# Carrying a batch's sums to all partition quadrants by sixteen SBUF-to-SBUF transfers instead of matmuls

## The chip, the cores and the metric

One Trainium2 (trn2) chip, one core. The metric is the device time of one execution in microseconds (us). Each kernel was run several times, in the same rounds and on the same chip as the kernel before; medians are quoted with the lowest and highest run. A program on one core shows a mean granted TensorE clock for each run, as a share of full speed.

## The reference

A polynomial-sketch attention feeds a SwiGLU feed-forward block. Cut to what matters:

```python
# q, k, v: (4 batches, 4 heads, 1088 positions, 32), float32; S1, S2: (8, 32)
def phi(x):                                  # 64 features per position and head
    a = einsum('rd,bhsd->bhsr', S1, x)
    b = einsum('rd,bhsd->bhsr', S2, x)
    return einsum('bhsi,bhsj->bhsij', a, b).reshape(..., 64)
q_p, k_p = phi(q), phi(k)
kv  = einsum('bhsf,bhsd->bhfd', k_p, v)      # per batch: values' sums, 64 x 32 per head
z   = sum(k_p, axis=2)                       # per batch: features' sums, 64 per head
num = einsum('bhsf,bhfd->bhsd', q_p, kv)
den = einsum('bhsf,bhf->bhs', q_p, z)[..., None] + 1e-06
x   = (num / den) as (4352, 128)
g, val = x @ w_gate, x @ w_val               # 128 -> 1536
out = (silu(g) * val) @ w_out                # 1536 -> 128
```

`kv` and `z` of a batch need all its positions, so nothing of `num` and `den` can start before them. `S1`, `S2` and the three weights reach the kernel as 64-bit numbers (the 8 x 32 values of `S1` are a load of 2 KB); the kernel turns them into float32 itself, which is called narrowing below.

## The kernel before

The feed-forward part is the bulk of the work. A block of 384 or 320 positions and one of 12 chunks of 128 hidden columns is a *unit*: two matmuls (`g`, `u`), a silu on ScalarE, a multiplication on VectorE (`hj`). A down-projection follows two units later. `g` and `u` take their PSUM banks from a rotation.

```python
    free_banks = ["g0", "g1", "g2", "acc"]
    turn = [0]
    def bank(tag=None):
        if tag is None:
            tag = free_banks[turn[0] % len(free_banks)]
            turn[0] += 1
        return psum.tile([P, TB], FP32, tag=tag, name="bank")
    # ... (cut)
    def unit(i, j, late=False):
        t0, n = blocks[i]
        g, u = bank(), bank()
        for o, w in ((g, wg), (u, wv)):
            nc.tensor.matmul(o[:, 0:n], w[:, j, :], xT[:, t0 : t0 + n], start=True, stop=True)
        # ... (cut) sg = silu(g) on ScalarE; hj = sg * u on VectorE, or on GpSimd for late ones
```

While the units of batch b run, the attention of batch b + 1 is worked off beside them, as a generator: after each unit it gets one turn, up to its next `yield`. This is the part that is changed, in the middle of it:

```python
        zs = feature_sums(phk)                       # sums over the position chunks, GpSimd
        # ... (cut: three yields)
        kvz = wide("a")
        key_values(kvz[:, 0, :], phk, 0, NC)         # kv: head h on partitions 32h..32h+31
        nc.tensor.matmul(kvz[:, 1, 0 : H * F], ones[:], zs, start=True, stop=True)  # z, 128 wide
        kvs = apool.tile([P, 2, 4, 32], FP32, tag="kvs", name="kvs")
        zrep = apool.tile([P, H * R, R], FP32, tag="zrep", name="zrep")
        nc.scalar.copy(kvs[:], ...)                  # kv, repeated four times
        nc.scalar.copy(zrep[:], ...)
        # ... (cut: load of the next batch's v)
        yield
        kvp = wide("b")[:, 0, 0 : 2 * P].rearrange("p (g n) -> p g n", g=2)
        for g in range(2):                           # turned and carried to all quadrants
            nc.tensor.matmul(kvp[:, g, :], kvs[:, g, :, :].rearrange("p a f -> p (a f)"),
                             ident[:], start=True, stop=True)
        kvr = apool.tile([P, 2, P], FP32, tag="kvr", name="kvr")
        nc.scalar.copy(kvr[:], kvp)
        # ... (cut) VectorE: zrep times query factors, sums, 1/den, query features, transpose phT
        # ... (cut) TensorE: num[quadrant] from kvr and phT;  copies of num into xT
```

In the last section of the first batch the rotation loses its fourth bank, which becomes the accumulator of the down-projections:

```python
    for z, (i, j) in enumerate(seq):
        if z == 17:
            free_banks.pop()
        unit(i, j)
        # ... (cut)
```

## Time and profile before

| | kernel before |
|---|---|
| time, median of 4 runs | 310.79 us (310.68 to 312.23) |
| span of the profiled run | 308.8 us |
| mean granted TensorE clock | 1.0 |
| TensorE busy | 302.3 us, 98% |

A line of the timeline gives start, duration, engine, source line, operation, names and shapes, and in brackets the idle time ahead of it with what ended that. A matmul's printed duration includes its modelled end, so read its pace from the next start. This is the timeline of the kernel before at the place of the change, in the first of the three later batches:

```profile
72.29 1.21 PE L312 MATMUL a<-phk,vld 128*32 128x64 f32 x72
73.43 0.70 PE L529 MATMUL a<-zs,ones 128*128 128x256 f32 x2
...
75.69 0.61 PE L543 MATMUL b<-ident,kvs 128*128 128x128 f32 x4
...
76.33 0.38 ACT L548 COPY kvr<-b 128x256 f32<-128x256 f32 x1 [1.18 <-PE b L543]
76.39 0.92 DVE L559 TENSOR_TENSOR phq<-zrep,qab 128x768 f32<-128x768 f32 x1
```

From the sums' end (73.97) to VectorE's first product with them (76.39) it takes 2.4 us, and TensorE never stands for it.

### The profile page before, as it was taken

Reading aid. Unit: us, or ns where it says so; the run is one execution under the profiler, and the core shown is the slowest. Engines: PE = TensorE matmul, PEld = TensorE weight load, DVE = VectorE, ACT = ScalarE, POOL = GpSimd, SP = SyncE. Lnnn points to the kernel's source line nnn. Section 1 sums busy time; section 2 is a strip of 40 time slices with the busy share of each in tenths; the row PEclk is TensorE's granted clock in tenths of the full one; section 3 lists DMA queues with packets and bytes.
Section 4 is the critical chain, followed back from the end, with each engine's and each line's share of the span. In section 5 each row is a group of like instructions: output and inputs, shape, how many; then the busy total and the mean of one; then the engine's idle time right before and its main releaser. Section 6 shows DMA issues by size and latency. Waiting matters only on the chain.

```text
span 308.8 us, 5147 instructions
## 1 busy us (share of the span) xinstructions
PE 302.3 (98%) x2066; PEld 191.1 (62%) x2066; DVE 175.7 (57%) x332; ACT 96.4 (31%) x227; POOL 37.3 (12%) x54
## 2 busy tenths in 40 slices
PE   8899999999999999999999999999999999999994
PEld 7545555656565566666666656655676655676664
DVE  4897999653659556279944552897532323333321
ACT  3556665223002313222232232322222222222230
POOL 3226223244000002400000032000000000000000
PEclk9999999999999999999999999999999999999999
DMA  7564390402111040220100100100010100100101
GB/s 197 165 168 104 103 318 0 146 0 70 31 28 21 2 132 14 34 66 0 27 2 0 24 1 2 25 0 0 11 17 0 21 2 1 25 0 1 22 0 26
DMA packets 24663, 13.96 MB, mean 45 GB/s; under 512 B 18368, under 2 KB 22720, under 8 KB 24640
## 3 DMA queue, kind: packets, MB, share of 16 engines
q1 hardware_dynamic: 23712, 13.28, 17.0%
q10 hardware_dynamic: 928, 0.36, 0.5%
q8 instruction: 16, 0.26, 0.4%
q14 instruction: 7, 0.06, 0.1%
HBM read 11.41 MB, written 2.23 MB: 44 GB/s over the span
## 4 chain that ended last, share of the span: by engine, by line
PE 89%; DVE 6%; ACT 2%; issue 1%; DVEq 0%
PE bank L652 50%; PE bank L680 28%; DVE hj L666 2%; PE bank L195 2%; DVE exp L225 1%; PE a L603 1%; PE a L278 1%; PE a L312 1%; DVE man L229 1%; PE b L278 1%; DVE exp L217 1%; PE a L694 1%; ACT exp L222 1%; PE a L529 1%; PE bank L325 0%
## 5 line engine op out<-in xcount | busy, mean ns | idle before, releaser
L666 DVE TENSOR_TENSOR hj<-sg,bank 128x384 f32<-128x384 f32 (+1 forms) x138 | 72.7, 528 | 102.3 <-PE bank L652 101.3
L658 ACT ACTIVATE sg<-bank 128x384 f32<-128x384 f32 (+1 forms) x144 | 67.8, 473 | 155.4 <-PE bank L652 155.4
L652 PE MATMUL bank<-xT,wg 128*128 128x384 f32 (+1 forms) x288 | 112.9, 474 | 0.0
L652 PE MATMUL bank<-xT,wv 128*128 128x384 f32 (+1 forms) x288 | 111.7, 469 | 0.3 <-DVE wv L238 0.3
L680 PE MATMUL bank<-hj,wo 128*128 128x384 f32 (+2 forms) x288 | 105.2, 460 | 0.2 <-DVE hj L666 0.2
L652 PEld LDWEIGHTS bank<-xT,wv 128*128 128x128 f32 x288 | 54.1, 190 | 34.5 <-DVE hj L666 2.7
L680 PEld LDWEIGHTS bank<-hj,wo 128*128 128x128 f32 x288 | 54.4, 190 | 32.9 <-issue 0.7
L652 PEld LDWEIGHTS bank<-xT,wg 128*128 128x128 f32 x288 | 53.1, 190 | 31.5 <-issue 2.4
L475 POOL TENSOR_TENSOR zs<-phk 128x1024 f32<-128x1024 f32 x3 | 7.0, 2349 | 111.9 <-PE bank L652 104.2
L566 DVE TENSOR_REDUCE dot<-phq 128x96 f32<-128x768 f32 x9 | 13.8, 1531 | 0.0
L301 DVE TENSOR_TENSOR phk<-kas,a 128x512 f32<-128x512 f32 (+1 forms) x12 | 8.7, 749 | 5.2 <-ACT kas L510 5.2
L708 DVE STREAM_TRANSPOSE o<-bank 128x384 f32<-128x384 f32 (+2 forms) x12 | 6.6, 548 | 6.9 <-PE bank L680 6.6
L222 ACT ACTIVATE exp<-exp,rebias 128x384 int32<-128x384 int32 (+3 forms) x15 | 8.3, 552 | 5.2 <-DVE exp L217 4.6
L590 DVE STREAM_TRANSPOSE phT<-phq 128x768 f32<-128x768 f32 x9 | 8.7, 967 | 0.1
L301 DVE TENSOR_TENSOR phq<-qab 128x768 f32<-128x768 f32 x9 | 8.5, 948 | 0.0
L559 DVE TENSOR_TENSOR phq<-zrep,qab 128x768 f32<-128x768 f32 x9 | 8.5, 942 | 0.0
L225 DVE SCALAR_TENSOR_TENSOR exp<-raw,exp 128x384 int32<-128x384 int32 (+2 forms) x14 | 7.4, 528 | 0.4 <-ACT exp L222 0.4
L621 ACT COPY xT<-a 128x64 f32<-128x64 f32 (+4 forms) x9 | 2.4, 333 | 15.8 <-PE b L603 9.5
L229 DVE SCALAR_TENSOR_TENSOR man<-raw,man 128x384 f32<-128x384 uint32 (+2 forms) x14 | 7.1, 511 | 0.0
L223 ACT ACTIVATE man<-man 128x384 f32<-128x384 int32 (+3 forms) x15 | 6.7, 450 | 0.0
L217 DVE TENSOR_SCALAR exp<-raw 128x384 int32<-128x384 int32 (+2 forms) x14 | 6.4, 457 | 0.5 <-DMA raw<-in_moe_w_val_dram 0.5
L263 DVE STREAM_TRANSPOSE kT<-kld 128x384 f32<-128x384 f32 (+2 forms) x9 | 6.1, 692 | 0.3 <-DMA kld<-in_k_dram 0.3
(113 smaller groups left out, 162.6 us busy)
## 6 DMA issues: line engine op xcount, KB each, us to landing
kld<-in_k_dram SPq DMA_DIRECT2D x4, 544.0 KB, 4.1
vld<-in_v_dram SPq DMA_DIRECT2D x12, 144.0 KB, 4.8
qld<-in_q_dram SPq DMA_DIRECT2D x3, 544.0 KB, 3.4
raw<-in_moe_w_out_dram SPq DMA_DIRECT2D x4, 384.0 KB, 4.0
out_dram<-o SPq DMA_DIRECT2D x28, 48.0 KB, 1.8
raw<-in_moe_w_gate_dram SPq DMA_DIRECT2D x3, 384.0 KB, 3.3
raw<-in_moe_w_val_dram SPq DMA_DIRECT2D x3, 384.0 KB, 3.4
out_dram<-o SPq DMA_DIRECT2D x16, 40.0 KB, 1.7
```

The source lines that it names most:

```text
L217: nc.vector.tensor_scalar(e[:], hi, 0x7FF00000, None, op0=ALU.bitwise_and)
L222: nc.scalar.activation(e[:], e[:], AF.Relu, bias=rebias[: shape[0], :], scale=8.0)
L225: nc.vector.scalar_tensor_tensor(out=e[:], in0=hi, scalar=-(1 << 31), in1=e[:], op0=ALU.bitwise_and, op1=ALU.bitwise_or,)
L229: nc.vector.scalar_tensor_tensor(out=f, in0=lo, scalar=2.0**-52, in1=f, op0=ALU.mult, op1=ALU.add)
L301: engine.tensor_tensor(out=phk[:, c0:c1, :, :, :].rearrange("p c h i j -> p (c h) i j"), in0=ka.unsqueeze(3).to_broadcast([P, n, R, R]), i ...
L559: nc.vector.tensor_tensor(out=prod, in0=zrep[:].unsqueeze(1).to_broadcast([P, n, H * R, R]), in1=fac.unsqueeze(3).to_broadcast([P, n, H * ...
L566: nc.vector.tensor_reduce(out=dot[:, x, :], in_=phq[:, c0:c1, :, :, :].rearrange("p c h i j -> p (c h) j i"), axis=AX.X, op=ALU.add,)
L590: nc.vector.transpose(out=phT[:, :, :, c0:c1, :].rearrange("p h g c t -> p c (h g) t"), in_=phq[:, c0:c1, :, :, :].rearrange("p c h (g i) ...
L652: nc.tensor.matmul(o[:, 0:n], w[:, j, :], xT[:, t0 : t0 + n], start=True, stop=True)
L658: nc.scalar.activation(sg[:, 0:n], g[:, 0:n], AF.Silu)
L666: nc.vector.tensor_tensor(out=hj[:, 0:n], in0=sg[:, 0:n], in1=u[:, 0:n], op=ALU.mult)
L680: nc.tensor.matmul(acc[i][:, 0:n], wo[:, j, :], hidden[i, j][:, 0:n], start=(j == 0), stop=(j == NCH - 1),)
```

## The change

The intent: TensorE is the bound, so take the carrying off it. The features' sum is made per head on 32 output columns and lands beside `kv`. VectorE turns `kv`, and sixteen transfers on the SyncE queue copy each head's sums to each of the four partition quadrants. To give these time, the attention waits four turns instead of one. In the first batch fewer warm-up matmuls on constants run (`keep_warm`), a mask and a matmul are put earlier, the later narrowing of weights is spaced wider, and the weight loads move from ScalarE's queue to SyncE's. The last output leaves in four transfers instead of two.

```diff
-        nc.tensor.matmul(kvz[:, 1, 0 : H * F], ones[:], zs, start=True, stop=True)
-        (kvs, zrep and their two ScalarE copies)
+        for h in range(H):
+            nc.tensor.matmul(
+                kvz[32 * h : 32 * h + 32, 1, 0:F], ones[:], zs[:, F * h : F * h + F],
+                start=True, stop=True,
+            )
+        kz4 = apool.tile([P, 2, F], FP32, tag="kz4", name="kz4")
+        spread = apool.tile([P, 2, H, F], FP32, tag="spread", name="spread")
+        nc.scalar.copy(kz4[:, 0, :], kvz[:, 1, 0:F])
+        nc.vector.transpose(
+            out=kz4[:, 1, :].rearrange("p (g d) -> p g d", g=2),
+            in_=kvz[:, 0, 0:F].rearrange("p (g f) -> p g f", g=2),
+        )
+        for a in range(4):
+            for h in range(H):
+                nc.sync.dma_start(
+                    out=spread[32 * a : 32 * a + 32, :, h, :],
+                    in_=kz4[32 * h : 32 * h + 32, :, :],
+                )
-        yield
-        (the two carrying matmuls and the copy to kvr)
+        for _ in range(4):
+            yield
 ... (cut: zrep and kvr become views of spread)
 first batch:
-    keep_warm(16, 32, ps=ps)
+    keep_warm(7, 32, ps=ps)
-    for _ in range(2):
-        load_next(nc.scalar)
 ... (cut: all these loads on SyncE now)
-    nd = totals(steps[1][1], phq, kvz, side_by_side("b"))
-    part("wv", 1)
-    unit(0, 1, late=True)
+    nd = side_by_side("b")
+    turn[0] = 2
+    unit(0, 1, late=True, between=(lambda: totals(steps[1][1], phq, kvz, nd), None))
-        z += z // 2 * 3
-        for at in (z, z + 1, z + 2 + z % 5):
+        z += z // 2 * 4
+        for at in (z, z + 1, z + 2 + z % 6):
 ... (cut: one more warm-up matmul, xT's layout for the last block, the last output)
```

More of the change, by code (lines that the diff above doesn't have):

```diff
@@ L137, with load_next @@
     coming += [("wo", i) for i in range(len(pieces["wo"]))]
-    def load_next(queue=nc.sync):
+    def load_next():
         if not coming:
@@ L149, in load_next @@
         if not wide_w:
-            queue.dma_start(out=dst[:, c0:c1, :], in_=part)
+            nc.sync.dma_start(out=dst[:, c0:c1, :], in_=part)
             return
         t = raw[name, i] = stage.tile([P, 3, P], I64, tag="raw", name="raw", bufs=NRAW)
-        queue.dma_start(out=t[:, 0 : c1 - c0, :], in_=part)
+        nc.sync.dma_start(out=t[:, 0 : c1 - c0, :], in_=part)
     nc.sync.dma_start(out=sraw[0:R, :], in_=S1)
@@ L168 @@
     ident = const.tile([P, P], FP32, name="ident")
-    ones = const.tile([P, P], FP32, name="ones")
+    ones = const.tile([P, Dh], FP32, name="ones")
     own = const.tile([P, H], FP32, name="own")
@@ L326, in unit_sums @@
                 kz[32 * a : 32 * a + 32, 0 : H * F],
-                ones[:, 0:Dh],
+                ones[:],
                 phk[:, c, :, :, :].rearrange("p h i j -> p (h i j)"),
@@ L459, in divide @@
             todo = [(xs, nd[0][:, :, 0:w].rearrange(deep, t=32), rs)]
-        if t0 == blocks[LAST][0]:
-            m = SPLIT // 64
-            ys = xT[:, t0 + SPLIT : t0 + BW].rearrange("p (t x a) -> p a x t", a=2, t=32)
-            _, num, r = todo.pop()
-            todo = [(xs[:, :, 0:m], num[:, :, 0:m], r[:, :, 0:m]), (ys, num[:, :, m:], r[:, :, m:])]
         for x, num, r in todo:
@@ L528, in attention @@
         key_values(kvz[:, 0, :], phk, 0, NC)
-        nc.tensor.matmul(kvz[:, 1, 0 : H * F], ones[:], zs, start=True, stop=True)
-        kvs = apool.tile([P, 2, 4, 32], FP32, tag="kvs", name="kvs")
-        zrep = apool.tile([P, H * R, R], FP32, tag="zrep", name="zrep")
-        nc.scalar.copy(
-            kvs[:],
-            kvz[:, 0, 0:F].rearrange("p (g f) -> p g f", g=2).unsqueeze(2).to_broadcast([P, 2, 4, 32]),
-        )
-        nc.scalar.copy(zrep[:], kvz[:, 1, 0 : H * F].rearrange("p (x r) -> p x r", r=R))
+        for h in range(H):
[9 more added lines that the diff above has]
+            in_=kvz[:, 0, 0:F].rearrange("p (g f) -> p g f", g=2),
+        )
+        for a in range(4):
[4 more added lines that the diff above has]
+                )
         if b + 1 < B:
             load_v(b + 1, [nc.sync] * 4)
-        yield
-        kvp = wide("b")[:, 0, 0 : 2 * P].rearrange("p (g n) -> p g n", g=2)
-        for g in range(2):
-            nc.tensor.matmul(
-                kvp[:, g, :], kvs[:, g, :, :].rearrange("p a f -> p (a f)"), ident[:],
-                start=True, stop=True,
-            )
-        kvr = apool.tile([P, 2, P], FP32, tag="kvr", name="kvr")
-        nc.scalar.copy(kvr[:], kvp)
+        for _ in range(4):
+            yield
+        zrep = spread[:, 0, :, :].rearrange("p h (i j) -> p (h i) j", j=R)
+        kvr = spread[:, 1, :, :].rearrange("p h (g d) -> p h g d", g=2)
         phq = apool.tile([P, NC, H, R, R], FP32, tag="phqs", name="phq")
@@ L560, in attention @@
                     out=prod,
-                    in0=zrep[:].unsqueeze(1).to_broadcast([P, n, H * R, R]),
+                    in0=zrep.unsqueeze(1).to_broadcast([P, n, H * R, R]),
                     in1=fac.unsqueeze(3).to_broadcast([P, n, H * R, R]),
@@ L604, in attention @@
                             num[a // 2][32 * h : 32 * h + 32, a % 2, 0 : 32 * n],
-                            kvr[r, g, 32 * h : 32 * h + 32],
+                            kvr[r, h, g, :],
                             phT[r, h, g, s0 : s0 + n, :],
@@ L610, in attention @@
             for u, engine in enumerate((nc.scalar.copy, nc.vector.tensor_copy)):
-                for c0, c1 in query_runs(b, s0, s1):
+                for c0, c1 in query_runs(s0, s1):
                     if c1 == NC and u == 1:
@@ L614, in attention @@
                     t0 = S * b + P * c0
-                    pat = "p (c a t) -> p a c t"
-                    if b == B - 1 and (c0, c1) == LASTC:
-                        pat = "p (c t a) -> p a c t"
                     wd = 4 if c1 < NC else 2
-                    dst = xT[:, t0 : t0 + 32 * wd * (c1 - c0)].rearrange(pat, a=wd, t=32)
+                    dst = xT[:, t0 : t0 + 32 * wd * (c1 - c0)].rearrange(
+                        "p (c a t) -> p a c t", a=wd, t=32
+                    )
                     src = num[u][:, :, 32 * (c0 - s0) : 32 * (c1 - s0)]
@@ L624, in attention, with query_runs @@
             yield
-    LASTC = ((blocks[LAST][0] % S + SPLIT) // P, (blocks[LAST][0] % S + SPLIT) // P + 1)
-    def query_runs(b, s0, s1):
-        cuts = {s0, s1}
-        cuts |= {c for c in (NC - 1,) if s0 < c < s1}
-        if b == B - 1:
-            cuts |= {c for c in LASTC if s0 < c < s1}
-        cuts = sorted(cuts)
-        return list(zip(cuts, cuts[1:]))
+    def query_runs(s0, s1):
+        cuts = [s0, NC - 1, s1] if s0 < NC - 1 < s1 else [s0, s1]
+        return zip(cuts, cuts[1:])
     LAG = 2
@@ L645, with unit @@
     lates = []
-    def unit(i, j, late=False):
+    def unit(i, j, late=False, between=(None, None)):
         t0, n = blocks[i]
@@ L651, in unit @@
         for o, w in ((g, wg), (u, wv)):
+            if between[0] and w is wv:
+                between[0]()
             nc.tensor.matmul(
@@ L662, in unit @@
         if late:
+            if between[1]:
+                between[1]()
             nc.scalar.copy(hj[:, 0:n], u[:, 0:n])
@@ L757 @@
     nc.scalar.copy(sq[:, 1, :, :], sTv[:, 1, :].unsqueeze(1).to_broadcast([P, R, R]))
-    for _ in range(2):
-        load_next(nc.scalar)
-    load_q(0, 2 * XS, 4 * XS)
-    for _ in range(2, NRAW if wide_w else len(coming) + 2):
+    for i in range(NRAW if wide_w else len(coming)):
+        if i == 2:
+            load_q(0, 2 * XS, 4 * XS)
         load_next()
@@ L795 @@
     part("wg", 1)
+    part("wv", 1)
     ps = bank("g0")
@@ L814 @@
     turn[0] = 2
-    keep_warm(1, ps=wide("a")[:, 0, :])
     divide(0, *steps[0], nd, among=("wg", "wv"))
     att = attention(1, ((0, 3), (3, NC)))
-    unit(0, 0, late=True)
+    unit(0, 0, late=True, between=(None, lambda: part("wv", 1)))
     part("wg", 1)
@@ L824 @@
     part("wv", 1)
-    part("wv", 1)
-    nd = totals(steps[1][1], phq, kvz, side_by_side("b"))
-    part("wv", 1)
-    unit(0, 1, late=True)
+    nd = side_by_side("b")
+    turn[0] = 2
+    unit(0, 1, late=True, between=(lambda: totals(steps[1][1], phq, kvz, nd), None))
     divide(0, *steps[1], nd)
@@ L910 @@
     b, x0 = divmod(t0 // 32, NX)
-    dst = out.rearrange("(b pp x) d -> b pp x d", pp=32, x=NX)[b, :, x0 : x0 + P // 32, :]
-    for i, queue in enumerate((nc.sync, nc.scalar)):
-        queue.dma_start(out=dst[16 * i : 16 * i + 16], in_=o[64 * i : 64 * i + 64, :])
+    dst = out.rearrange("(b pp x) d -> b x pp d", pp=32, x=NX)[b]
+    for i in range(P // 32):
+        queue = nc.scalar if i % 2 else nc.sync
+        queue.dma_start(out=dst[x0 + i], in_=o[32 * i : 32 * i + 32, :])
 _INS = ["q", "k", "v", "S1", "S2", "moe_w_gate", "moe_w_val", "moe_w_out"]
```

## The prediction

> **What bounds the kernel now.** I read the busy line and the chain of the page first.
>
> ```profile
> PE 302.3 (98%) x2066; PEld 191.1 (62%) x2066; DVE 175.7 (57%) x332; ACT 96.4 (31%) x227; POOL 37.3 (12%) x54
> ...
> PE 89%; DVE 6%; ACT 2%; issue 1%; DVEq 0%
> ```
>
> TensorE is busy 98% of the span and is 89% of the chain that ended last. "Busy" is no proof, since matmuls are pipelined, so I read start times in the timeline: matmuls of 384 columns start 0.645 us apart (two passes of 0.3225), those of 320 columns 0.54. The feed-forward part runs at that pace nearly everywhere, and TensorE's list of waits has only six entries, together about 2.3 us, one of them later than 40 us. So from about 19.6 us to 304.9 us the time is the sum of TensorE's work; a matmul saved there is time saved, and a wait put there is time lost. Two stretches differ. Up to 19.6 us TensorE waits for the first batch's sums and for narrowed weights. From 30 to 50 us VectorE is nearly as full as TensorE:
>
> ```profile
> 15.00:20.00 5.00, 4.56 (x48) 2.01 (x42) 4.52 (x15) 3.20 (x8) 1.70 (x3) 1.00 0.75 215
> ...
> 45.00:50.00 5.00, 5.00 (x17) 2.65 (x16) 5.00 (x11) 2.80 (x7) 2.03 (x2) 1.00 0.21 65
> ```
>
> (The windows view; columns are us, then busy us of TensorE, its weight loads, VectorE, ScalarE, GpSimd.) Adding up the matmuls between 19.59 and 50.53 us at their own pace gives about 29.3 us, so 1.6 us of slip hide there as slightly late starts. I blame about 1.2 us of it on VectorE.
>
> The parts to be replaced, from the groups of TensorE by form:
>
> ```profile
> L529 PE MATMUL a<-zs,ones 128*128 128x256 f32 x6 | 2.1, 431 | 0.0
> L543 PE MATMUL b<-ident,kvs 128*128 128x128 f32 x12 | 1.8, 274 | 0.0
> ```
>
> In the timeline of the first such batch the sums start at 73.43 and the next matmul at 73.97 (0.54 us); the two carrying matmuls start at 75.69 and the next at 76.13 (0.44 us).
>
> **What the Trainium skill says.** "TensorE: Matmul & The Clock Gate", Part 3, says that matmuls with 32 output columns put on different column groups run at the same time. The trace agrees: 72 passes of 64 columns (line 312) take 1.14 us from first start to the next instruction, 16 ns each, while a 384-column pass at full width costs 0.84 ns a column, so 54 ns for 64. "TensorEngine Tiling (Array Packing)", Key Properties, says a change of tiling mode drains the array: part of the 0.54 us above is that (two passes of 256 columns are 0.43 us), and it stays. "DMA: Bandwidth & Descriptors", Rules for kernel authors, says transfers under 64 KB are mostly overhead and should be merged. Each new transfer is 32 x 2 x 64 x 4 bytes = 16 KB; the trace's smallest comparable ones show the overhead (below). Its section "Issuing engines are not separate DMA queues" calls the sequencer's issue time usually small beside the transfer; here, with sixteen in a row on one queue, I expect the issue time to be the larger part.
>
> **The change part by part.**
>
> (1) TensorE's work in batches 1 to 3. The 128-wide sum becomes four 32-wide ones of 64 columns on four column groups: 8 passes x 16 ns = 0.13 us, plus the unchanged drain of 0.11: 0.54 becomes about 0.24, saving 0.30. The two carrying matmuls vanish: 0.44. So 0.74 us a batch, 2.2 us in all, all of it on the path.
>
> (2) The carry. The program's order shows: TensorE's sums, a ScalarE copy (about 0.22 us), then a VectorE transpose that waits for that copy (about 0.26), then sixteen transfers on the SyncE queue, and VectorE's first product waits for all of them. The queue's rate, from its own timeline:
>
> ```profile
> 123.50 1.90 SPq L714 DMA_DIRECT2D out_dram<-o  x4
> 129.86 1.75 SPq L130 DMA_DIRECT2D vld<-in_v_dram  x4
> ```
>
> and the landing time, from the list of issues:
>
> ```profile
> out_dram<-o SPq DMA_DIRECT2D x16, 40.0 KB, 1.7
> ```
>
> Both kinds are transfers of 32 partitions with three dimensions, as the new ones are: 0.46 us each to issue, 1.7 to 1.8 to land. From the end of the sums I count 0.2 + 0.22 + 0.06 + 0.26 + 0.1 + 15 x 0.46 + 1.8 = 9.5 us. Against that the change puts four feed-forward units between sums and first use. A unit is 3 x 0.645 = 1.93 us, so 7.7 us plus 0.4 until VectorE gets there: VectorE should stand about 1.5 us at the first product in batches 2 and 3. A multiplication result may be about 1.5 us late before TensorE lacks a PSUM bank, so most of this is absorbed.
>
> (3) Everything behind the carry moves three units later. Per later batch the attention now asks for 28 turns instead of 25 of the 36 units. For batch 3 there is room. For batch 2 there is not: the 9 turns left over from batch 1 and 28 make 37. Its last matmuls (line 603, `num`) and the copies into xT, which before ran with five units to spare, now come after the last unit of batch 1, right before the matmul that reads xT; the order listing confirms it. The cost there, from the rows of the same work in the kernel before:
>
> ```profile
> 155.51 0.49 DVE L666 TENSOR_TENSOR hj<-sg,bank 128x320 f32<-128x320 f32 x1 [0.24 <-PE bank L652]
> 155.87 0.43 PE L603 MATMUL a<-phT,kvr 32*32 32x288 f32 x2
> ...
> 157.37 0.81 PE L652 MATMUL bank<-xT,wg 128*128 128x320 f32 x2
> 157.47 0.70 ACT L621 COPY xT<-a 128x512 f32<-128x512 f32 x2 [2.14 <-PE a L603]
> 157.53 0.69 DVE L621 COPY xT<-b 128x512 f32<-128x512 f32 x1 [1.54 <-PE a L603]
> ```
>
> After the last unit VectorE does its multiplication (0.27 after the end, 0.41 long) and a transpose (0.97), then `num` may start: 1.75 us, of which 0.54 is covered by one down-projection: 1.2 us idle. Then `num` ends, the VectorE copy takes 0.69 plus 0.15 and 0.08 of hand-over: 0.9 us idle. Together 2.1 us. VectorE's lag of (2), not all worked off among the 320-wide units (VectorE needs some 1.6 of 1.61 us there), adds about 1.1 us as small waits. I replayed these queues in order with the durations above; batches 1 and 2 of feed-forward come out 1.7 us longer than before (0.6 at 0.35 us an issue, 2.4 at 0.5), the saving of the two batches prepared in them included. The third saving, 0.74 us, falls in the first batch: there the product waits until about 83.2 us instead of 76.4, but the transposes end about 89.2 and TensorE reaches `num` at 89.7, so it is free by a narrow margin.
>
> (4) The first batch. Masks of the second value weights are made early and the second unit's first matmul is put ahead of the `totals` (1.3 us), so its second matmul, which waited for the weight until 19.59 us, should start near 18.85. The unit after next then waits for xT from VectorE, so about 0.6 of the 0.74 us remain. The later narrowing spaced wider takes about 2 us of VectorE out of the full stretch: I take 0.4 us of the 1.2. The dropped warm-up matmuls (0.2 to 0.3 us) buy at most 0.1, since kT and the weight on GpSimd come next. Sum: about -1.0 us, plausible -0.2 to -1.8.
>
> (5) The end. Four output transfers instead of two, two on each queue: the second of a queue leaves about 0.2 us later. +0.2.
>
> Sum: 310.7 + 1.7 - 0.74 - 1.0 + 0.2 = 310.9. I add 0.2 for hand-overs not counted, eight semaphores before one product among them: **311.1 us**.
>
> **Rivals.** (a) The transfers hide wholly and the batch-2 boundary is cheaper (0.35 us an issue, as the plain 2-D weight loads show): saved matmuls and first batch win, near 309.4. Against it: every 32-partition row shows 0.44 to 0.48. (b) The transfers become the bound: at 0.6 us an issue and 2.2 us landing VectorE stands almost 4 us, PSUM banks run out in both batches, the first batch loses its margin: 314 to 316. For it: sixteen in one queue beside stores and loads; against it: the DMA share is under 0.2 after 93 us. (c) The first batch, not the carry, decides: VectorE falls short between 20 and 50 us and the early gain is eaten, near 312.
>
> **Range and chances.** (a) sets the lower end, (c) and half of (b) the upper: 309.3 to 313.3. A change of 2% is 6.2 us; faster would need nearly three times the saved matmuls, slower needs all of (b). Faster 0.01, same 0.95, slower 0.04.
>
> **What would show it.** Right: TensorE 0.24 instead of 0.54 us at the sums and no carrying matmul; sixteen issues over about 7 us; a VectorE wait on the transfers of 1 to 2 us; an idle TensorE of about 2 us before the first unit of batch 2 (some 165 us) and none before batch 3; the first unit pair earlier by 0.6 us. Wrong: a pace of the queue far from 0.46 us, idle TensorE inside batches, or a first batch that is no shorter.

## The result, and the profile after

The changed kernel takes **322.66 us** (321.37 to 324.19, 4 runs) against 310.79. The ratio is 1.0375, 95% interval 1.0327 to 1.0423: slower. The prediction was 311.1 with 313.3 as its upper end; the measured time is 11.6 us above the first. The profiled run's span is 319.6 us, 10.8 longer than before.

The page of the kernel after (busy line, granted clock in 40 slices, chain by engine and by line):

```profile
PE 302.0 (94%) x2062; PEld 190.7 (60%) x2062; DVE 173.9 (54%) x333; ACT 93.7 (29%) x219; POOL 37.0 (12%) x54
...
PEclk9999999999989999999799999999999999999999
...
PE 79%; SPq 9%; DVE 5%; DMA 3%; issue 2%; ACT 0%; DVEq 0%
PE bank L647 50%; PE bank L677 20%; SPq L539 9%; DMA spread<-kz 2%; DMA kld<-in_k_dram 1%; PE a L603 1%; PE a L278 1%; PE a L312 1%; PE b L278 1%; DVE dot L566 1%; PE a L691 1%; DVE phT L590 1%; DVE hj L663 1%; PE bank L325 0%; PE bank L278 0%
```

Line 539 issues the new transfers; its queue (SPq) is now 9% of the chain that ended last, and their landing 2% more. TensorE is busy as long as before in a longer span, and in two slices its clock is not full. The timeline of the kernel after, at the place of the change, first TensorE, ScalarE, VectorE:

```profile
71.89 1.21 PE L312 MATMUL a<-phk,vld 128*32 128x64 f32 x72
72.92 0.29 PE L524 MATMUL a<-zs,ones 128*32 128x64 f32 x8
73.15 0.81 PE L647 MATMUL bank<-xT,wg 128*128 128x320 f32 x2
73.28 0.21 ACT L532 COPY kz<-a 128x64 f32<-128x64 f32 x1 [2.03 <-PE a L524]
73.53 0.25 DVE L533 STREAM_TRANSPOSE kz<-a 128x64 f32<-128x64 f32 x1 [1.62 <-ACT kz L532]
...
85.48 0.96 DVE L559 TENSOR_TENSOR phq<-spread,qab 128x768 f32<-128x768 f32 x1 [8.68 <-DMA spread<-kz]
```

then the SyncE queue, in the first of the later batches (the other two take 10.38 us each):

```profile
73.81 10.35 SPq L539 DMA_DIRECT2D spread<-kz  x16
```

The sums cost TensorE 0.23 us instead of 0.54, and the carrying matmuls are gone. But sixteen transfers take 10.35 us to issue, about 0.645 us from one to the next. From the sums' end at 73.15 to VectorE's first product at 85.48 it is now 12.3 us. What TensorE waits for in the kernel after (us in total, times, longest; the kernel before had none of these four):

```profile
PE bank L647 <- DVE hj L663: 5.1, 3, 2.5
PE a L603 <- DVE phT L590: 3.5, 2, 2.5
...
PE bank L677 <- DVE o L705: 1.0, 1, 1.0
PE bank L647 <- DVE xT L620: 0.9, 1, 0.9
```

VectorE stands 8.7, 4.5 and 4.3 us for the transfers (17.5 in all) and is then late with everything in its order: the transposes `phT` before `num`, the multiplications `hj`, the output transpose `o`. And after the two longest of these stands, 2.5 us each, the clock falls. TensorE's timeline after 91 us, and the windows view (us, then busy time of TensorE, weight loads, VectorE, ScalarE, GpSimd, then the granted clock, DMA share, GB/s):

```profile
91.83 0.27 PE L603 MATMUL a<-phT,spread 32*32 32x96 f32 x2 [2.50 <-DVE phT L590]
...
94.52 1.49 PE L647 MATMUL bank<-xT,wg 128*128 128x384 f32 x2
95.80 1.25 PE L647 MATMUL bank<-xT,wv 128*128 128x384 f32 x2
96.89 0.81 PE L647 MATMUL bank<-xT,wg 128*128 128x384 f32 x2
```

```profile
93.00:94.00 1.00, 1.00 (x4) 0.56 (x4) 0.22 (x1) 0.12 (x1) 0.00 (x0) 0.64 0.00 0
94.00:95.00 1.00, 1.00 (x3) 0.66 (x2) 0.23 (x1) 0.00 (x0) 0.00 (x0) 0.50 0.00 0
95.00:96.00 1.00, 1.00 (x3) 0.54 (x2) 1.00 (x2) 0.00 (x0) 0.00 (x0) 0.50 0.00 0
...
155.00:156.00 1.00, 1.00 (x3) 0.64 (x2) 1.00 (x3) 0.00 (x0) 0.00 (x0) 0.50 0.47 70
```

The same two passes start 1.28 us apart at half clock instead of 0.645. The Trainium skill, "TensorE: Matmul & The Clock Gate", Part 1, names an idle window of about 3.4 us as what sends the clock to half, in a window that runs free of the kernel. Here 2.5 us without a matmul, then 0.9 us of small 32x32 ones, went before it. Before the second spell (154.9 to 158 us) it was 2.5 us without a matmul, 1.3 us of full ones and another 1.0 us without. By the windows each spell loses about 1.7 us, 3.4 together. The same stand is not always followed by one: in `contig` (below), whose carry is as slow, half clock came at 174 to 178 us after the two stands of 1.0 and 0.9 us at the start of batch 2's block, where the kernel after kept the full clock, and none came after the stand of 2.2 us in batch 1. The four runs of the kernel after have mean clocks of 0.988, 0.989, 0.984 and 0.981, the two lowest in the two longest runs.

**Theories.** (A) *The queue*: the pace of the transfers makes VectorE late, TensorE idles, and the clock loss comes on top. (B) *The units*: the four yields themselves, which leave batch 2's attention no room before its block, cost the time whatever carries the sums. (C) *The first batch*: its reordering lost something. Then, inside (A): is the pace one of bytes, of the shape, or of where the transfer reads and writes? And how much is idle, how much clock?

### The profile page after: what moved, and what is told of

It reads as the page before. It is cut to its first block, busy times and chain, and to the rows that moved or that the text cites. A ratio compares the mean times of both kernels' runs of the same rounds, so it can differ in the third digit from the quotient of the medians.

```text
span 319.6 us, 5203 instructions
## 1 busy us (share of the span) xinstructions
PE 302.0 (94%) x2062; PEld 190.7 (60%) x2062; DVE 173.9 (54%) x333; ACT 93.7 (29%) x219; POOL 37.0 (12%) x54
## 4 chain that ended last, share of the span: by engine, by line
PE 79%; SPq 9%; DVE 5%; DMA 3%; issue 2%; ACT 0%; DVEq 0%
PE bank L647 50%; PE bank L677 20%; SPq L539 9%; DMA spread<-kz 2%; DMA kld<-in_k_dram 1%; PE a L603 1%; PE a L278 1%; PE a L312 1%; PE b L278 1%; DVE dot L566 1%; PE a L691 1%; DVE phT L590 1%; DVE hj L663 1%; PE bank L325 0%; PE bank L278 0%
## 5 line engine op out<-in xcount | busy, mean ns | idle before, releaser
L647 PE MATMUL bank<-xT,wg 128*128 128x384 f32 (+1 forms) x288 | 114.2, 479 | 6.1 <-DVE hj L663 5.1
L677 PE MATMUL bank<-hj,wo 128*128 128x384 f32 (+2 forms) x288 | 106.5, 465 | 1.0 <-DVE o L705 1.0
L647 PEld LDWEIGHTS bank<-xT,wg 128*128 128x128 f32 x288 | 53.9, 192 | 39.7 <-DVE hj L663 7.3
L647 PEld LDWEIGHTS bank<-xT,wv 128*128 128x128 f32 x288 | 55.0, 192 | 34.7 <-issue 1.0
L559 DVE TENSOR_TENSOR phq<-spread,qab 128x768 f32<-128x768 f32 x9 | 8.5, 945 | 17.5 <-DMA spread<-kz 17.5
L620 ACT COPY xT<-a 128x64 f32<-128x64 f32 (+3 forms) x7 | 2.3, 367 | 24.0 <-PE b L603 16.6
L603 PE MATMUL a<-phT,spread 32*32 32x288 f32 (+2 forms) x128 | 5.3, 352 | 3.5 <-DVE phT L590 3.5
L603 PEld LDWEIGHTS a<-phT,spread 32*32 32x32 f32 x128 | 2.9, 103 | 6.2 <-DVE phT L590 5.0
```

Of the source, the lines that this page charges most:

```text
L559: nc.vector.tensor_tensor(out=prod, in0=zrep.unsqueeze(1).to_broadcast([P, n, H * R, R]), in1=fac.unsqueeze(3).to_broadcast([P, n, H * R, R]),
L603: nc.tensor.matmul(num[a // 2][32 * h : 32 * h + 32, a % 2, 0 : 32 * n], kvr[r, h, g, :], phT[r, h, g, s0 : s0 + n, :], start=(g == 0), st ...
L677: nc.tensor.matmul(acc[i][:, 0:n], wo[:, j, :], hidden[i, j][:, 0:n], start=(j == 0), stop=(j == NCH - 1),)
```

## The experiments

Twelve kernels were run. All results are correct except that of `pace`, which is wrong.

### Is it the carry at all? carry_back and carry_alone

`carry_back` is the kernel after with the carry of the kernel before (one yield, matmuls, ScalarE copies); everything else stays changed. `carry_alone` is the opposite: the kernel before with only the carry changed.

```diff
 carry_back (against after)
-        (four 32-wide sums, kz4, sixteen dma_start, four yields)
+        nc.tensor.matmul(kvz[:, 1, 0 : H * F], ones[:], zs, start=True, stop=True)
+        (kvs, zrep, yield, two carrying matmuls, kvr, as in the kernel before)
 carry_alone (against before): the same lines the other way
```

> The changed kernel with the carry alone undone: the two matmuls and the 128-wide sum carry the sums again, and the three later turns are gone. Queue theory (the sixteen transfers leave 0.645 us apart, so the carry takes 12.3 us against 8.1 us of cover, VectorE stands, then TensorE stands and its clock drops) and boundary theory (the three later turns do it): 310.3 us, between 309.8 and 311. First-batch theory (reordered loads and narrowing do it): 316 us or more.

> The kernel before with the carry alone changed. Queue theory and boundary theory: 321 to 324 us, VectorE waiting 8.7, 4.5 and 4.3 us for the transfers as in the changed kernel. First-batch theory: 311 to 313 us.

Measured: `carry_back` 309.70 us (309.59 to 309.89), ratio to before 0.9962 (0.9947 to 0.9977), clock 0.999 to 1.0. `carry_alone` 323.35 us (322.74 to 323.65), ratio 1.0398 (1.0382 to 1.0413). TensorE's waits in `carry_alone`:

```profile
PE bank L658 <- DVE hj L672: 4.7, 2, 2.4
PE a L609 <- DVE phT L596: 3.2, 2, 2.2
```

They are the waits of the kernel after, and `o` and `xT` follow with 1.0 and 0.9 as there. So the carry costs 322.66 - 309.70 = 13.0 us (12.6 by `carry_alone`), and the rest of the change wins 310.76 - 309.70 = 1.1. (C) is out.

### Queue or units? two_queues, act_queue and room

`two_queues` halves the queue's work and leaves all else: every second quadrant's transfers are issued by GpSimd. `act_queue` gives them to ScalarE. `room` leaves the queue and gives batch 2's attention three more turns in batch 1.

```diff
 two_queues                                        (act_queue: nc.scalar)
-                nc.sync.dma_start(
+                (nc.gpsimd if a % 2 else nc.sync).dma_start(
                     out=spread[32 * a : 32 * a + 32, :, h, :],
 room
-            next(att, None)
+            for _ in range(2 if b == 1 and 9 <= z < 12 else 1):
+                next(att, None)
```

> The changed kernel with every second quadrant's four transfers issued by GpSimd instead of SyncE. Queue theory: eight transfers a queue leave within 5.2 us, all have landed some 7.5 us after the sums, VectorE's waits fall from 8.7, 4.5 and 4.3 us to about 3.6, 0 and 0; what stays is the boundary of batch 2: 311.5 to 313.5 us, if GpSimd issues as fast as SyncE. If the transfers themselves and not their issue were slow: 320 us or more, the waits unchanged.

> The same split, with ScalarE issuing the second half. Queue theory: the waits for the transfers shorten as with GpSimd, but ScalarE cannot start a Silu for some 5 us, so hj comes late and TensorE waits for it once a batch, 2 to 3 us each: 315 to 320 us.

> The changed kernel, where batch 2's attention gets three turns more inside batch 1, so that its last matmuls and copies stand two units ahead of the first matmul of batch 2 again. Boundary theory: 312 to 315 us. Queue theory: only the 1.9 us idle at the boundary go, 320 to 321.5 us, and VectorE's three waits for the transfers stay at 8.7, 4.5 and 4.3 us.

Measured, `two_queues`: **309.78 us** (308.85 to 310.54), ratio 0.9953 (0.9914 to 0.9991). The queue of SyncE and, in a second view, GpSimd's:

```profile
74.00 5.26 SPq L539 DMA_DIRECT2D spread<-kz  x8
```

```profile
74.29 4.39 POOL L539 DMA_DIRECT2D spread<-kz  x8 [1.07 <-DVE kz L533]
```

The first product starts at 80.58. VectorE waits for the transfers in one batch only, 3.6 us, and TensorE does not feel it. Two of its three waits left after 40 us stand at the boundary of batch 2 (the third, 0.7 us for `hj` in the first batch, is treated below):

```profile
PE a L603 <- DVE phT L590: 1.0, 1, 1.0
PE bank L647 <- DVE xT L620: 0.9, 1, 0.9
```

So 12.9 us are won back by halving the queue alone, with the four yields in place: (A), not (B). What (B) stands for is these 1.0 + 0.9 us. The time is below the 311.5 to 313.5 that I had expected, so the gain was underrated.

`act_queue`: 327.14 us (326.59 to 328.04), ratio 1.0506, worse than one queue. That was a miss: I had expected 315 to 320. ScalarE's timeline shows why:

```profile
73.79 5.54 ACTq L539 DMA_DIRECT2D spread<-kz  x8
79.38 0.77 ACT L653 ACTIVATE sg<-bank 128x320 f32<-128x320 f32 x2 [5.90 <-DMA spread<-kz]
```

The silu of the units stands 5.9 us behind the eight issues in ScalarE's own order, and TensorE waits 12.2 us in three places for a PSUM bank (`sg` in its list of waits). Which engine issues matters as much as how many issues there are: GpSimd had nothing of the feed-forward part to do then, ScalarE serves every unit.

`room`: 318.57 us (316.68 to 319.72), 4.1 us under the kernel after, where the queue theory had put it at 320 to 321.5. VectorE's waits for the transfers are unchanged (17.9 us). Gone from TensorE's list are the second `phT` (1.0), `o` (1.0) and `xT` (0.9), together 2.9. The other 1.2 us is within the scatter of both kernels, whose clock losses vary from run to run (0.987 to 0.995 here); I did not settle it.

### What sets the pace? contig and pace

`contig` makes each transfer plain: 512 bytes in a row for each partition on both sides, two dimensions.

```diff
-        spread = apool.tile([P, 2, H, F], FP32, tag="spread", name="spread")
+        spread = apool.tile([P, H, 2, F], FP32, tag="spread", name="spread")
-                    out=spread[32 * a : 32 * a + 32, :, h, :],
-                    in_=kz4[32 * h : 32 * h + 32, :, :],
+                    out=spread[32 * a : 32 * a + 32, h, :, :].rearrange("p t f -> p (t f)"),
+                    in_=kz4[32 * h : 32 * h + 32, :, :].rearrange("p t f -> p (t f)"),
```

`pace` measures other transfers at the same place. It gives a wrong result: batch 1's sixteen read HBM (32 partitions x 512 bytes), batch 2's read SBUF but a quarter of the bytes, batch 3's are four of 128 partitions.

```diff
+                if b == 1:
+                    nc.sync.dma_start(out=flat[rows, cols], in_=k[0, h]...[0:32, :])
+                elif b == 2:
+                    nc.sync.dma_start(out=flat[rows, 2*F*h : 2*F*h + 32],
+                                      in_=ident[32*h : 32*h + 32, 0:32])
+                elif h == 0:
+                    nc.sync.dma_start(out=flat[:, 2*F*a : 2*F*a + 2*F], in_=ident[:])
```

> The changed kernel with the destination laid out so that each of the sixteen transfers writes one run of 512 bytes in a partition instead of two of 256, both sides two-dimensional. If the shape of the transfer sets the 0.645 us: pace 0.4 to 0.47 us, the waits of VectorE in batches 2 and 3 fall from 4.4 to 1 to 2 us, 312 to 315 us. If every transfer with both sides in SBUF takes 0.645 us: nothing changes, 321 to 324 us.

> Wrong results on purpose; measures what sets the 0.645 us of a transfer on SyncE. Batch 1: the same sixteen 32 x 128 transfers, but read from HBM. Batch 2: sixteen from SBUF with a quarter of the bytes (32 x 32). Batch 3: four from SBUF over all 128 partitions. If having both sides in SBUF sets the pace: 0.33 to 0.48 us in batch 1, about 0.6 in batches 2 and 3. If bytes or runs set it: 0.6 in batch 1, clearly under 0.5 in batch 2. If it is the 32 partitions: under 0.5 only in batch 3.

Measured: `contig` 322.66 us (320.93 to 324.41), ratio 1.0378, sixteen issues in 10.1 to 10.8 us: no difference, the shape is not it. `pace` (one run of 308.58 us, state unknown, so only its queue is read), SyncE's queue in three places:

```profile
73.23 7.45 SPq L543 DMA_DIRECT2D spread<-in_k_dram  x16
...
131.28 10.85 SPq L548 DMA_DIRECT2D spread<-ident  x16
...
187.45 2.48 SPq L553 DMA_DIRECT2D spread<-ident  x4
```

From HBM it is 0.466 us each, just the pace that the prediction used. From SBUF it is 0.678 us each with a quarter of the bytes (one of the sixteen took 1.31, the median is 0.59 and then a gap of some 0.04), and 0.62 with four times the partitions. Stores, which read SBUF and write HBM, take 0.47 (the four of 1.88 us that the trace of before shows at 76.50). So among transfers at this place the issue was slow where both ends lie in SBUF, whatever the size, shape and partition count. It is not the only slow kind: at the end of the trace of before, one store of 64 partitions to HBM shows

```profile
305.26 0.66 SPq L913 DMA_DIRECT2D out_dram<-o_last  x1
```

while the two stores of 32 partitions each that replace it on that queue take 0.80 together in the kernel after. Why an issue is slow is not shown by any of these runs.

### How much is the clock? warm

The kernel after with matmuls on constants put where TensorE would stand; the transfers and VectorE's waits are untouched.

```diff
+                if b > 1 and c0 == 0:                 # after the first product of batches 2, 3
+                    keep_warm(11 if b == 2 else 8, ps=wide("b")[:, 0, :])
+            if b == 1 and s0 == 0:                    # before num of batch 1
+                keep_warm(11, ps=wide("b")[:, 0, :])
```

> The changed kernel with 8 to 11 idle-time matmuls of 512 columns on constants placed where TensorE stands for the carry (before num in the first batch, after the second unit behind the first product in batches 2 and 3). If the dips of the granted clock come from TensorE's idle time: clock back to 0.995 or more, and 317 to 319.5 us, since a mean clock of 0.986 over 321 us is 4.5 us of lost clock. If not: clock stays below 0.99 and the time is 321 us or more.

Measured: 318.92 us (317.51 to 319.56), ratio 1.0242 (1.0202 to 1.0281), clock 0.999 to 1.0. VectorE still waits 17.6 us. TensorE's timeline where the kernel after was at half clock:

```profile
90.65 2.57 PE L195 MATMUL b<-const-bfloat16-1.0 128*32 128x512 bf16 x11
94.18 1.34 PE L681 MATMUL bank<-hj,wo 128*128 128x320 f32 x4
95.36 0.81 PE L651 MATMUL bank<-xT,wg 128*128 128x384 f32 x2
96.00 0.81 PE L651 MATMUL bank<-xT,wv 128*128 128x384 f32 x2
```

The passes are 0.64 us apart again. Work that nobody needs made the kernel 322.66 - 318.92 = 3.7 us faster. That is the clock's share, near the 3.4 that the windows gave; the other 318.92 - 309.78 = 9.1 us over `two_queues` is mostly TensorE standing for late data. The list of waits of the kernel after has 7.9 us of it: 10.5 in the four lines above, less the 0.7 in the first batch and the 1.9 at the boundary, which `two_queues` has too. The other 1.2 I cannot assign.

### The bank in the first batch, and a faster version: turn_fix, two_room, best, best_g0

In the kernel after and in `carry_back` TensorE stood 0.7 us near 48.6 us for `hj`. The change's second `turn[0] = 2` moves the count of the bank rotation; where the rotation narrows from four banks to three, `g` of the next unit gets bank g1, which `u` of the unit before has just been given. `turn_fix` sets the count there, on top of `carry_back`. `two_room` joins `two_queues` and `room`. `best` is `two_room` with that setting, and `best_g0` starts the rotation one bank further on.

```diff
         if z == 17:
             free_banks.pop()
+            turn[0] = 2            # turn_fix, best: next banks g2, g0  (best_g0: turn[0] = 0: g0, g1)
```

> The kernel after with the matmul carry of before, as in carry_back (309.70 us against a before of 310.76), and one more edit: where the fourth PSUM bank leaves the rotation of the feed-forward part, the counter of the rotation is set so that the next two banks are g2 and g0. If the 0.7 us by which TensorE stood for VectorE's multiplication near 48.6 us came from the rotation handing out a bank that was just used, that wait goes, the first batch's end comes about 0.7 us earlier and the time is about 309.0 us, 0.6 to 0.7 under carry_back's. If VectorE was late there by itself (it is nearly full between 30 and 50 us), the wait only moves a unit later and the time stays at 309.7.

> The kernel after with every second one of the sixteen transfers issued by GpSimd (two_queues: 309.78 us, before 311.01) and three more turns of the attention for batch 2 in batch 1 (room). With the carry of the two queues hidden, the only idle left by the delay of four units is the boundary before batch 2, 1.0 us before the numerators and 0.9 us before the first unit. If that is the price of the extra units alone, it goes and the time is about 307.9 us, 1.9 under two_queues. If the earlier turns push VectorE behind, new waits for its multiplication appear and less than 1 us is won.

> two_room with the edit of turn_fix: two queues for the transfers, room for batch 2's attention, and the rotation of the PSUM banks set at its narrowing. If the three costs are independent, 309.8 minus 1.9 minus 0.7: about 307.2 us, a ratio near 0.988 of before, with no wait of TensorE over 0.5 us after 40 us and a granted clock of 1.0. If they overlap, 307.5 to 309.

> two_room with the rotation of the PSUM banks set to begin with g0 where it narrows, so that u of the next unit, not g, gets the bank just used, and the last unit of the first batch leaves u in g1. In turn_fix and best the wait near 48.6 us went, but a wait of 0.65 us for the multiplication of the last unit came near 76 us, since block 1's sums take bank g0 and the shifted rotation had put that unit's u there. If both 0.7 us waits are the rotation's, none over 0.3 us stays after 40 us here, and the time is about 306.4 us, 0.6 under two_room (307.0). If VectorE is simply late in the first batch, a wait of about 0.7 us stays and the time is 307.0.

| kernel | median us (range) | ratio to before (95%) |
|---|---|---|
| turn_fix | 309.68 (309.48 to 310.74) | 0.9966 (0.9943 to 0.9988) |
| two_room | 307.01 (306.75 to 308.14) | 0.9876 (0.9855 to 0.9898) |
| best | 307.00 (306.71 to 308.18) | 0.9874 (0.9851 to 0.9896) |
| best_g0 | **306.47** (306.42 to 307.66) | 0.9851 (0.9826 to 0.9876) |

`turn_fix` was a miss: no gain. The wait near 48.6 us went, and batch 1's key sums came at 70.86 instead of 71.72 us, but then this appeared in TensorE's timeline of `turn_fix`:

```profile
76.60 8.54 PE L671 MATMUL bank<-hj,wo 128*128 128x384 f32 x26 [0.65 <-DVE hj L657]
```

Block 1's down-projections accumulate in the fixed bank g0, and the shifted rotation had given g0 to `u` of the last unit. `best` kept this wait too (0.7 us), though its expectation had none over 0.5. With `best_g0`, which avoids both meetings, neither wait is in TensorE's list, and the median is 0.54 us under `two_room`. The two ranges overlap and they ran on different chips (before: 310.81 and 310.95), so the traces carry this point more than the medians. `two_room` won 2.8 us over `two_queues`, 1.9 of it the boundary's waits, which are gone from its list; the other 0.9 I cannot assign.

## Why the prediction was right or wrong

**Where the 11.9 us came from.** The runs in a row, each a difference of medians, on up to three chips whose before agrees within 0.3 us:

| from | to | us | what |
|---|---|---|---|
| before, 310.76 | carry_back, 309.70 | -1.1 | first batch and end |
| carry_back | two_queues, 309.78 | +0.1 | matmuls saved, boundary paid |
| two_queues | warm, 318.92 | +9.1 | queue too slow: TensorE stands (7.9 listed) |
| warm | after, 322.66 | +3.7 | clock lost in those stands |

**The bound** was read right. TensorE's busy time stayed at 302 us in both profiles, and the rest of the span rose from 6.5 to 17.6 us; that the busy time did not fall with the matmuls saved fits the spells of half clock.

**Step (1), TensorE's work**, was right: 0.23 us at the sums against a predicted 0.24, no carrying matmul, 2.2 us in all. They are there in `two_queues`, offset by the boundary.

**Step (2), the carry, is the step that failed**, by one term: "0.46 us each to issue", taken from stores and loads as the "comparable" ones. It measured 0.645. The other terms held: ScalarE's copy 0.21, VectorE's transpose 0.25, the landing 1.8. So the carry took 12.3 us instead of 9.5, against about 8.1 us of cover, and VectorE stood 4.5 and 4.3 us in batches 2 and 3 instead of 1.5. The rows used as a model had the right partitions and dimensions, but one end in HBM, and `pace` shows that this is what counts: 0.466 from HBM, 0.62 to 0.68 with both ends in SBUF. No transfer in the trace before had both ends in SBUF, so its true pace could not be read there. The text relied on the likeness instead of leaving that step open. The rows were also read too well. A row's mean hides a short first issue: the four stores shown start at 123.50, 123.89, 124.41 and 124.92, so the later ones leave 0.51 us apart. And "every 32-partition row shows 0.44 to 0.48" is not so: the four loads at 73.56, at the very place of the change, took 2.37 us, and the four stores at 148.59 took 2.14.

**The step from VectorE's wait to TensorE** was right as a mechanism. "A multiplication result may be about 1.5 us late before TensorE lacks a PSUM bank": with waits of 4.5 and 4.3 instead of 1.5, TensorE stood 2.5 + 1.0 and 1.9 us. The first batch "is free by a narrow margin": the product came 2.3 us later than the assumed 83.2, the margin was gone, and `num` stood 2.5 us. These stands are the 7.9 us above.

**The granted clock was not in the prediction at all.** No rival named it either, and it is 3.7 of the 13 us. The mean clock of the kernel before is 1.0, so its trace does not show it.

**Step (3), the boundary of batch 2**, was right: 2.1 us predicted, 1.0 + 0.9 measured, and its cause (no turns left) is confirmed by `room` and `two_room`.

**Step (4), the first batch**: its -1.0 and the end's +0.2, so -0.8, came out as -1.1 in `carry_back`, which is in part luck: the parts did not all hold. The second unit's second matmul started at 19.02 us instead of the predicted 18.85 (before 19.59). The VectorE stretch gave less, because of the 0.7 us bank wait, which I did not see: I had looked at the order of instructions, not at which bank each gets. The key sums of batch 1 came only 0.4 us earlier in the kernel after and 0.6 in `carry_back`; where the rest of the 1.1 was won was not tested.

**Step (5), the end**: no cost was found; from the last copy's end to the end of the span it is about 3.4 us after and 3.6 before.

**The rivals.** (b) named what happened: 0.6 us an issue, VectorE standing almost 4 us, banks running out in both batches, the first batch's margin lost. It gave 314 to 316 and stopped short of the clock and of some of the idle time; its 2.2 us of landing did not come (1.8). It was argued down with the low share of the DMA engines, 0.2 after 93 us. That was the wrong view: the limit is the rate at which one engine issues, and a DMA engine's share does not show it. In `two_queues` SyncE kept its pace, eight in 5.26 us, with eight more beside it on GpSimd. The Trainium skill, "DMA: Bandwidth & Descriptors", Issuing engines are not separate DMA queues, says that several engines' queues only save the sequencer's issue time, usually small beside the transfer. The runs agree with what is saved; but here it was not small, it was worth 12.9 us. (a) and (c) did not happen. The chance of 0.04 for slower was too low, since one unmeasured number carried the whole step.

## What to carry to other kernels

A row of small transfers that gates a product costs its number of issues times the issue time, so measure that time for the same kind of source and destination before counting on cover. Split such a row over two issuing engines, and give the second half to one that the critical work doesn't need in that stretch. Fewer, larger transfers were not tried as a carry; `pace` issued four of 128 partitions in 2.48 us. When TensorE is the bound, count a stand of 2.5 us at more than its length, because here half clock followed both of them, and when the number of PSUM banks in a rotation changes, check which bank the next two tiles get.

## What the Trainium skill lacked or had wrong

- "DMA: Bandwidth & Descriptors" has no issue time per transfer that depends on where its two ends lie. On SyncE's queue it was 0.466 us from HBM, 0.47 for stores to HBM, and 0.62 to 0.68 with both ends in SBUF, at 4, 16 and 64 KB alike; one store of 64 partitions to HBM took 0.66 as well. For eight in a row with both ends in SBUF: 5.26 us on SyncE, 5.54 on ScalarE, 4.39 on GpSimd.
- The same page, Issuing engines are not separate DMA queues, calls the issue time that several engines save usually small. Here the sixteen issues took 10.35 us against 1.8 us of landing, and splitting them won 12.9 us (GpSimd). That section does not say that an engine's own work stands behind its issues: ScalarE's silu stood 5.9 us, and the kernel was 4.5 us slower than with one queue.
- The Trainium skill, "TensorE: Matmul & The Clock Gate", Why this matters for your kernels, allows idle gaps up to about 3 us. Here half clock followed 2.5 us without a matmul and 0.9 us of 32x32 ones, and filling the gaps won 3.7 us. It varied from run to run: a stand of 1.9 us before 213.7 us was followed by full clock, and in `contig` two of 1.0 and 0.9 us near 174 us were followed by half clock.
